# Summing the heads' logits on VectorE by way of DRAM instead of with selector matmuls, in a kernel bound by TensorE

## Chip, cores, metric

One core of one Trainium2 chip. The metric is device time in microseconds (us); lower is better. The engines are called PE (TensorE), DVE (VectorE), ACT (ScalarE), POOL (GpSimd) and SP (the engine whose queue starts the DMA transfers). "Starts" of matmuls below are start times in the trace. Full-width matmuls (128 rows, 128 columns, 512 moved columns, bf16) that nothing delays start 216 ns apart, and eight of them make a group of 1.73 us. A **PE wait** is what a gap between two starts has beyond 216 ns; gaps of 432 ns where the trace lacks the record of one matmul (about every fiftieth of `acc_wo` and `dacc` in some profiles) are not counted.

## The reference

Two rounds of the same two layers on x of 2048 tokens by 1024 features, all bf16: a dilated sliding-window attention (32 heads of 32, window 8, dilation 2) and a gated MLP with 3584 hidden features. Both have a layernorm ahead and a residual. (Shortened; `...` marks what is left out.)

```python
def _A_ref(x, wqkv, wo):                 # H = 32, Dh = 32, W, dil = 8, 2
    q, k, v = ...                        # x @ wqkv, split by heads
    idx = pos[:, None] - (jnp.arange(W) * dil)[None, :]
    kg, vg = ...                         # k and v gathered at idx
    logits = jnp.einsum("bhsd,bhswd->bhsw", q, kg) * scale   # masked where idx < 0
    attn = softmax(logits, axis=-1)
    o = jnp.einsum("bhsw,bhswd->bhsd", attn, vg)
    return o.transpose(0, 2, 1, 3).reshape(B, S, D) @ wo

def _B_ref(x, W_gate, W_up, W_down):
    gate, up = x @ W_gate, x @ W_up
    return (relu(gate) * up) @ W_down

for _ in range(2):
    x = x + _A_ref(layernorm(x), wqkv, wo)
    x = x + _B_ref(layernorm(x), W_gate, W_up, W_down)
```

## The kernel before

A block is 512 tokens in one of the two rounds, so there are eight, numbered n = 0 to 7. PE goes through the stages in a fixed order: in the first part v of blocks 0 to 3, q and k of blocks 0 and 1, and the output projection of block 0; then for each n the gate/up stage of block n (28 pairs of groups `acc_g`, `acc_u`), q and k of block n+2 (from block 4 on also v), the output projection `acc_wo` of block n+1, and the down projection `dacc` of block n. The attention of block n+1 runs on DVE while PE does gate/up of block n. q and k are laid out with four features of each head next to one another on the 128 partitions. DVE multiplies q with shifted k and sums over eight chunks; then the four partitions of one head have to be added. Before, this was a matmul with a 0/1 matrix `sel` of 32 columns, in tiles of 128 by 32 (all code below is shortened; `...` marks larger cuts):

```python
psum   = tc.tile_pool(name="psum", bufs=6, space=PSUM)      # six accumulators, tag "acc"
psum_l = tc.tile_pool(name="psum_l", bufs=1, space=PSUM)    # two banks, for the logits L

def dv(f, *args, **kwargs):          # fixes DVE's order: behind the last one issued so
    with tc.issue_after(tail_dve[0]):
        tail_dve[0] = f(*args, **kwargs).ins

def red_mm(n, prod, first, last):    # eight selector matmuls
    for wh in range(2):
        for tq in range(TPB):
            mm(st["L"][32 * tq:32 * tq + 32, WH * wh:WH * (wh + 1), :], lhsT=sel[:],
               rhs=prod[:, WH * wh:WH * (wh + 1), tq * P:(tq + 1) * P],
               start=first, stop=last, tile_position=(0, 32 * tq), ...)
# block 0: one red_mm per chunk, eight groups. Blocks 1 to 7: DVE sums the chunks into s, one red_mm.

def softmax(n):
    nc.vector.tensor_reduce(m[:], Lt..., op=ALU.max)
    nc.vector.tensor_tensor(d[:], Lt[:], m..., op=ALU.subtract)
    nc.scalar.activation(d[:], d[:], ACT.Exp, scale=scale)
    nc.vector.tensor_reduce(ssum[:], d..., op=ALU.add)
    nc.vector.reciprocal(rs[:], ssum[:])
    nc.vector.tensor_tensor(a[:], d[:], rs..., op=ALU.mult)

# pv_steps: eight units of four DVE operations each: tt = a * v, three halving adds into ohm

# gate/up, step j of 28
for nm in ("g", "u"):
    acc = psum.tile([P, BLK], F32, tag="acc", name=f"acc_{nm}")
    ...                                                   # eight matmuls
    if nm == "g":
        r = pool["hid"].tile([P, BLK], BF16, tag="r", name="r", bufs=3)
        tail_act[0] = nc.scalar.activation(r[:], acc[:], ACT.Relu).ins
nc.vector.tensor_tensor(hold["hT"][:, j, :], accs["u"][:], r[:], op=ALU.mult)   # frees acc_u

# down projection
if s8 == 0:
    accs[half] = [psum.tile([P, BLK], F32, tag="acc", name=f"dacc{t}") for t, _, _ in cols]

# the plan for gate/up of block n >= 1 ("at" is the stage's start in planned us)
ev.append((at + 0.1, reds_n[n + 1]))
ev.append((at + 0.2, lambda n=n: softmax(n + 1)))
spread(pv_steps(n + 1), at + 12.0, 6.5)
```

The product hT(j) on DVE is what gives an up group's accumulator back to PE, and the ReLU on ACT is what gives a gate group's back. DVE's operations without `dv` are ordered by the scheduler at build time, which interleaves two units where it can.

Of the kernel before, what the change touches and what calls it, by code (L numbers as in the profile page):

```python
# [17 lines left out]
W = 8  # L18
# [18 lines left out]
def kernel(  # L37
# [117 lines left out]
    v_d = dram.tile([H * DH, NTOK], BF16, name="v_d")  # L155
    o_d = dram.tile([NT, H, DH, P], BF16, name="o_d")
    zpad = const.tile([P, KC, HALO], BF16, name="zpad")
    nc.gpsimd.memset(zpad[:], 0.0)
# [145 lines left out]
    def ln_first():  # L304
# [55 lines left out]
        def turn(t):  # L360
            tps[t] = psum.tile([P, KC, P], BF16, tag="acc", name="tp")
            for c in range(KC):
                with pe_group():
                    tail_pe[0] = nc.tensor.transpose(tps[t][:, c, :], xna[:, t, c * P:(c + 1) * P], ident[:]).ins

        def copy(t, eng, c0=0, c1=KC):
            f = nc.vector.tensor_copy if eng == "v" else nc.scalar.copy
            on(eng, f, hold["xnT"][:, t, c0:c1, :], tps[t][:, c0:c1, :])

# [12 lines left out]
        apply(1)  # L382
        copy(0, "v", 0, KC // 2)
        copy(0, "a", KC // 2, KC)
        turn(1)
        act_vpe(2, st1)
        copy(1, "v", 0, KC // 2)
        copy(1, "a", KC // 2, KC)
        bn(3, 0)
# [3 lines left out]
        apply(3)  # L393
        hold["later"] = {2: (lambda: (turn(2), copy(2, "a"))),
                         4: (lambda: (turn(3), copy(3, "v", 0, KC // 2), copy(3, "a", KC // 2, KC)))}
        return hold
# [109 lines left out]
    def prod_direct_steps(n):  # L506
        prods = {}

        def mult(c):
            def f():  # L510
                prods[c] = work.tile([P, W, BLK], BF16, tag="t", name=f"prod_{c}")
                i0, i1 = qk_bcast(n, c, 0, W)
                dv(nc.vector.tensor_tensor, prods[c][:], i0, i1, op=ALU.mult)
            return f

        def red(c):
            def f():
                red_mm(n, prods.pop(c), c == 0, c == KC - 1)
            return f

        return [mult(c) for c in range(KC)], [red(c) for c in range(KC)]

    def prod_sum_steps(n):
        st = att[n]

        def mult(h, c):
            def f():
                if h == 0 and c == 0:
                    st["s"] = big_tile([P, W, BLK], f"s_{n}")
                i0, i1 = qk_bcast(n, c, WH * h, WH)  # L530
                if c == 0:
                    t = work.tile([P, WH, BLK], F32, tag="ac", name=f"ac_{n}_{h}", bufs=1)
                    st["ac"] = t
                else:
                    t = work.tile([P, WH, BLK], F32, tag="t", name=f"t_{n}_{h}_{c}")
                    st[("t", c)] = t
                behind = gate[0] if n == 1 else down_gate[0] if n == 2 else None
                if behind is not None:
                    with tc.issue_after(behind):
                        nc.vector.tensor_tensor(t[:], i0, i1, op=ALU.mult)  # L540
                else:
                    nc.vector.tensor_tensor(t[:], i0, i1, op=ALU.mult)  # L542
                if c > 1:
                    add(h, c - 1)
                if c == KC - 1:
                    add(h, c)
            return f

        def add(h, c):
            ac, t = st["ac"], st.pop(("t", c))  # L550
            o = st["s"][:, WH * h:WH * (h + 1), :] if c == KC - 1 else ac[:]
            nc.vector.tensor_tensor(o, ac[:], t[:], op=ALU.add)  # L552

        def red():
            red_mm(n, st["s"], True, True)

        return [mult(h, c) for h in range(2) for c in range(KC)], red

    def softmax(n):
        st = att[n]  # L560
        Lt = st["L"]
        if n % NB == 0:
            reg = Lt[0:32, :, 0:HALO]
            nc.vector.tensor_tensor(reg, reg, maskc[:], op=ALU.add)
        m = soft.tile([P, P], F32, tag="m", name="m")
        nc.vector.tensor_reduce(m[:], Lt[:].rearrange("p w t -> p t w"), axis=AX.X, op=ALU.max)
        d = soft.tile([P, W, P], F32, tag="d", name="d")
        nc.vector.tensor_tensor(d[:], Lt[:], _ap(m, 0, [[0, W], [1, P]]), op=ALU.subtract)
        nc.scalar.activation(d[:], d[:], ACT.Exp, scale=scale)
        ssum = soft.tile([P, P], F32, tag="ssum", name="ssum")  # L570
        nc.vector.tensor_reduce(ssum[:], d[:].rearrange("p w t -> p t w"), axis=AX.X, op=ALU.add)
        rs = soft.tile([P, P], F32, tag="rs", name="rs")
        nc.vector.reciprocal(rs[:], ssum[:])
        a = soft.tile([P, W, P], BF16, tag="a", name=f"a_{n}", bufs=2)
        nc.vector.tensor_tensor(a[:], d[:], _ap(rs, 0, [[0, W], [1, P]]), op=ALU.mult)
        st["a"] = a

# [14 lines left out]
    def pv_steps(n):  # L592
# [3 lines left out]
        def f_(g):  # L596
            def f():
# [5 lines left out]
                v_sh = _ap(st["v_hm"], HALO + g * DG * (HALO + P), [[-DIL, W], [HALO + P, DG], [1, P]])  # L603
                nc.vector.tensor_tensor(tt[:], a_bc, v_sh, op=ALU.mult)  # L604
                nc.vector.tensor_tensor(tt[:, 0:4], tt[:, 0:4], tt[:, 4:8], op=ALU.add)  # L605
                nc.vector.tensor_tensor(tt[:, 0:2], tt[:, 0:2], tt[:, 2:4], op=ALU.add)
                gate[0] = nc.vector.tensor_tensor(ohm[:, g * DG:(g + 1) * DG, :], tt[:, 0], tt[:, 1], op=ALU.add).ins
            return f
# [46 lines left out]
    def gu_steps(n, ln):  # L655
        hold = {}

        def f_(j):
            def f():
# [4 lines left out]
                for nm in ("g", "u"):  # L664
# [6 lines left out]
                    if nm == "g":  # L671
                        r = pool["hid"].tile([P, BLK], BF16, tag="r", name="r", bufs=3)
                        tail_act[0] = nc.scalar.activation(r[:], acc[:], ACT.Relu).ins  # L673
                nc.vector.tensor_tensor(hold["hT"][:, j, :], accs["u"][:], r[:], op=ALU.mult)  # L674
            return f

        return [f_(j) for j in range(FC)], hold

    down_gate = [None]

    def down_steps(n, hold):
        b = n % NB
        accs = {}

        def f_(half, s8):
            def f():
                hT = hold["hT"]
                cols = [(t, 0, SLAB) for t in range(TPB)]
                if n == NN - 1 and half == 1:
                    cols[-1:] = [(TPB - 1, 0, SLAB // 2), (TPB - 1, SLAB // 2, SLAB)]  # L690
                if s8 == 0:
                    accs[half] = [psum.tile([P, BLK], F32, tag="acc", name=f"dacc{t}") for t, _, _ in cols]
                ac = accs[half]
# [8 lines left out]
                if s8 == NSL - 1:  # L702
                    for a, (t, c0, c1) in zip(ac, cols):
                        xt = x_tiles[b * TPB + t]
                        xs = xt[:, half * SLAB + c0:half * SLAB + c1]
                        ins = nc.vector.tensor_tensor(xs, a[:, c0:c1], xs, op=ALU.add).ins  # L706
                        if n == 0 and half == 0:
                            down_gate[0] = ins
                        if n == NN - 1:
# [26 lines left out]
    ln_b = {}  # L736
    reds_n = {}
    ln_a[0] = ln_first()
# [22 lines left out]

    GAP0 = 2.05
    t_v0 = 9.5
# [25 lines left out]
    for c in range(KC):  # L789
        ev.append((t_qk0 + GAP0 * (2 * c + 2.0), mults[c]))  # L790
        if c < KC - 2:
            ev.append((t_qk0 + GAP0 * (2 * c + 4.5), reds[c]))
    spread(load_v_steps(0), t_qk0 + 19.0, 1.0)
    ev.append((t_qk1 + 0.5 * GRP, reds[KC - 2]))
    ev.append((t_qk1 + 2.5 * GRP, reds[KC - 1]))
    ev.append((t_qk1 + 2.6 * GRP, lambda: softmax(0)))
    ln1(2, t_qk0 + 10.0, t_qk1 + 5.0, True, 4.5)
    spread(qk_steps(1, ln_a[1], "qk01"), t_qk1, GRP)
# [8 lines left out]
    ev.append((t_wo0 + 3.0, store_v(2)))  # L807
    sums1, red1 = prod_sum_steps(1)
    spread(sums1[:4], t_qk1 + 50.0, 4.4)
# [6 lines left out]
    spread(load_v_steps(1), t_gu0 + 6.0, 7.0)  # L816
    ev.append((t_gu0 + 58.1, red1))
    ev.append((t_gu0 + 58.2, lambda: softmax(1)))
    ev.append((t_gu0 - 0.01, start_hidden))

    at = t_gu0
    for n in range(NN):
# [3 lines left out]
        if n == 0:  # L826
            spread(pv_steps(1), at + 66.0, 5.5)
            ev.append((at + 105.0, store_o(1)))
            ev.append((at + 105.1, load_o(1)))
        elif n + 1 < NN:  # L830
            ev.append((at + 0.1, reds_n[n + 1]))
            ev.append((at + 0.2, lambda n=n: softmax(n + 1)))
            spread(pv_steps(n + 1), at + 12.0, 6.5)
            ev.append((at + 72.0, store_o(n + 1)))
            ev.append((at + 72.1, load_o(n + 1)))
        if n + 2 < NN:
            ln1(n + 2, at + 30.0, at + 58.0)
        at += 2 * GRP * FC
        if n + 2 < NN:
            want_qk(("qk", n + 2), at + 2 * GRP * KC)  # L840
            spread(qk_steps(n + 2, ln_a[n + 2], ("qk", n + 2)), at, GRP)
            sums, reds_n[n + 2] = prod_sum_steps(n + 2)
            spread(sums, at + GRP * (K_STEP[0] + 1.0), 4.4)
            at += 2 * GRP * KC
# [51 lines left out]
```

## Time and profile before

1629.85 us, median of four runs beside the changed kernel (1629.76 to 1630.19); 1629.79 in the runs that were there first. The profiled execution spans 1628.1 us.

| profile before | |
|---|---|
| PE busy | 1617.5 us, 99% |
| DVE busy | 1062.6 us, 65% |
| DMA queue q1 | 63.4% of 16 engines, 295 MB |
| first `acc_v` of the real work | 9.99 us (it waits for a weight load) |
| last matmul to the end | about 3.6 us |
| selector matmuls | 120, in 15 groups of eight |

From the page of the kernel before, its head, the first lines of its parts 1 and 4, the clock and the DMA queue:

```profile
span 1628.1 us, 18770 instructions
PE 1617.5 (99%) x7617; PEld 784.6 (48%) x7666; DVE 1062.6 (65%) x927; ACT 506.0 (31%) x1050; POOL 255.9 (16%) x220
...
PEclk9999999999999999999999999999999999999999
...
q1 hardware_dynamic: 371808, 295.23, 63.4%
...
PE 95%; DVE 4%; issue 1%; DMA 0%; SPq 0%; DVEq 0%
```

PE is busy 99% at full clock, and the chain that ended last runs over PE for 95%. Time is to be had only from PE: fewer matmuls, or fewer waits. The Trainium skill, "Trainium Kernel Development and Optimization", Performance Expectations, calls matmul busy time a bad metric because matmuls are pipelined. This trace agrees: a matmul is shown as 379 ns long and starts 216 ns after the one before it. All PE waits below are therefore read from starts.

The timeline of PE before, around one group of selector matmuls (block 1; columns: start, length of the run, engine, line, operation, tiles, count):

```profile
198.78 1.03 PE L129 MATMUL acc_u<-xnT_b,w_u 128*128 128x512 bf16 x4
199.73 0.61 PE L129 MATMUL L<-s,sel 128*32 128x512 bf16 x8
200.28 1.90 PE L129 MATMUL acc_g<-xnT_b,w_g 128*128 128x512 bf16 x8
```

From the first L matmul to the next group is 0.55 us, and the first L matmul itself starts 0.31 us after the last `acc_u` one, 0.09 more than usual: the group costs 0.65 us (0.64 by the rounded lines).

The timeline of PE before, in the down projection of block 0 (in brackets the idle time and what ended it):

```profile
305.83 1.67 PE L129 MATMUL dacc<-w_d,hT 128*128 128x512 bf16 x7
308.28 2.96 PE L129 MATMUL dacc<-w_d,hT 128*128 128x512 bf16 x12 [0.77 <-DVE x L706]
```

Seven matmuls should take 1.51 us from start to start and took 2.45: a wait of 0.94 us for an accumulator that DVE has not yet read. It is the largest PE wait after the start.

The DVE and then the ACT timeline before, at the start of gate/up of block 1 (`m` is the maximum over L, `d` is L minus m, then the Exp of `d` on ACT, `ssum` is the sum after it):

```profile
333.33 1.22 DVE L566 TENSOR_REDUCE m<-L 128x128 f32<-128x1024 f32 x1
334.58 1.22 DVE L568 TENSOR_TENSOR d<-L,m 128x1024 f32<-128x1024 f32 x1
336.82 0.69 DVE L674 TENSOR_TENSOR hT<-acc_u,r 128x512 bf16<-128x512 f32 x1 [1.02 <-PE acc_u L129]
337.43 1.91 DVE L571 TENSOR_REDUCE ssum<-d 128x128 f32<-128x1024 f32 x1
```

```profile
335.03 0.60 ACT L673 ACTIVATE r<-acc_g 128x512 bf16<-128x512 f32 x1 [3.51 <-PE acc_g L129]
335.83 1.06 ACT L569 ACTIVATE d<-d 128x1024 f32<-128x1024 f32 x1 [0.21 <-DVE d L568]
```

`d` is ready at 335.80, and the Exp starts at 335.83, after only 0.21 us in which ACT was idle: it stands after two ReLUs in ACT's order, just where its data comes.

### The profile page before, as it was taken

How to read it: one execution, taken by the hardware profiler on the slowest of the kernel's cores; microseconds unless marked ns; L12 is line 12 of the kernel's file. 1: busy time of each engine (PE TensorE's matmuls, PEld its weight loads, DVE VectorE, ACT ScalarE, POOL GpSimd, SP SyncE). 2: the span in 40 equal slices, each digit the busy share in tenths (PEclk: the TensorE clock that was granted, in tenths of full speed). 3: DMA queues.
4: the chain of work that ended last, by engine and by line, in shares of the span. 5: the costliest groups of instructions: out<-in, count | busy, mean ns of one | idle time of the engine just before them, and what ended most of it. 6: DMA issues, size and time to landing. Idle time of an engine off the chain costs nothing.

```text
span 1628.1 us, 18770 instructions
## 1 busy us (share of the span) xinstructions
PE 1617.5 (99%) x7617; PEld 784.6 (48%) x7666; DVE 1062.6 (65%) x927; ACT 506.0 (31%) x1050; POOL 255.9 (16%) x220
## 2 busy tenths in 40 slices
PE   9999999999999999999999999999999999999999
PEld 5644445444544445444454444544445444444444
DVE  5699899985497927949279492894818958211211
ACT  4754323243241513405134051331513311131110
POOL 2421003310250102201052010520105100000000
PEclk9999999999999999999999999999999999999999
DMA  9579656747476485664857648577484764655452
GB/s 304 91 203 256 164 175 201 193 156 196 140 215 175 155 233 168 184 177 149 230 180 185 185 150 224 165 200 215 147 229 158 198 203 155 206 160 177 156 167 67
DMA packets 372183, 296.83 MB, mean 182 GB/s; under 512 B 142592, under 2 KB 352896, under 8 KB 371200
## 3 DMA queue, kind: packets, MB, share of 16 engines
q1 hardware_dynamic: 371808, 295.23, 63.4%
q8 instruction: 60, 0.98, 0.3%
q10 hardware_dynamic: 288, 0.39, 0.1%
q14 instruction: 27, 0.22, 0.0%
HBM read 256.77 MB, written 21.00 MB: 171 GB/s over the span
## 4 chain that ended last, share of the span: by engine, by line
PE 95%; DVE 4%; issue 1%; DMA 0%; SPq 0%; DVEq 0%
PE acc_g L129 24%; PE acc_u L129 24%; PE dacc L129 22%; PE acc_v L129 7%; PE acc_k L129 6%; PE acc_q L129 6%; PE acc_wo L129 6%; DVE t L542 1%; DVE ac L552 1%; PE L L129 1%; DMA w_v<-in_A_wqkv_dram 0%; DVE pv L604 0%; DVE x L649 0%; DVE pv L605 0%; DVE ac L542 0%
## 5 line engine op out<-in xcount | busy, mean ns | idle before, releaser
L129 PE MATMUL acc_g<-xnT_b,w_g 128*128 128x512 bf16 x1792 | 423.4, 379 | 0.0
L129 PE MATMUL acc_u<-xnT_b,w_u 128*128 128x512 bf16 x1792 | 423.3, 379 | 0.0
L129 PE MATMUL dacc<-w_d,hT 128*128 128x512 bf16 (+1 forms) x1787 | 386.6, 376 | 2.5 <-DVE x L706 0.8
L673 ACT ACTIVATE r<-acc_g 128x512 bf16<-128x512 f32 x224 | 133.4, 596 | 747.1 <-PE acc_g L129 747.1
L674 DVE TENSOR_TENSOR hT<-acc_u,r 128x512 bf16<-128x512 f32 x224 | 153.7, 687 | 315.0 <-PE acc_u L129 313.5
L129 PEld LDWEIGHTS <-hT 128*128 128x128 bf16 x1820 | 178.0, 98 | 209.9 <-issue 1.1
L129 PEld LDWEIGHTS <-w_g 128*128 128x128 bf16 x1792 | 174.8, 98 | 212.8 <-issue 3.0
L129 PEld LDWEIGHTS <-w_u 128*128 128x128 bf16 x1792 | 175.3, 98 | 211.4
L552 DVE TENSOR_TENSOR ac<-ac,t 128x2048 f32<-128x2048 f32 x84 | 191.7, 2282 | 0.4
L542 DVE TENSOR_TENSOR t<-q,k 128x2048 f32<-128x2048 bf16 x81 | 184.8, 2290 | 8.5 <-ACT k L480 5.8
L485 POOL COPY kh<-k 128x14 bf16<-128x14 bf16 x64 | 81.4, 1276 | 472.0 <-ACT k L480 471.8
L706 DVE TENSOR_TENSOR x<-dacc,x 128x512 bf16<-128x512 f32 (+1 forms) x65 | 42.5, 679 | 164.0 <-PE dacc L129 164.0
L604 DVE TENSOR_TENSOR pv<-a,vhm 128x4096 bf16<-128x4096 bf16 x64 | 145.2, 2282 | 0.0
L129 PE MATMUL acc_wo<-w_o,oT 128*128 128x512 bf16 x496 | 111.0, 379 | 0.8
L245 POOL TENSOR_TENSOR st_b<-st_b,neg_half 128x1 f32<-128x1 f32 x29 | 56.5, 1956 | 288.7 <-ACT st_b L244 288.6
L245 POOL TENSOR_TENSOR st_a<-st_a,neg_half 128x1 f32<-128x1 f32 x32 | 41.9, 1316 | 319.2 <-ACT st_a L244 319.1
L484 POOL COPY k<-kh 128x14 bf16<-128x14 bf16 x48 | 70.5, 1469 | 65.9 <-DVE t L542 43.8
L129 PEld LDWEIGHTS <-oT 128*128 128x128 bf16 x512 | 50.1, 98 | 60.3
L605 DVE TENSOR_TENSOR pv<-pv 128x2048 bf16<-128x2048 bf16 x64 | 77.4, 1215 | 0.2
L476 ACT CAST q<-acc_q 128x512 bf16<-128x512 f32 x64 | 37.3, 583 | 73.3 <-PE acc_q L129 73.2
L240 ACT ACTIVATE xn_b<-x 128x1024 bf16<-128x1024 bf16 x29 | 30.3, 1045 | 89.3 <-DVE x L649 89.3
L480 ACT CAST k<-acc_k 128x512 bf16<-128x512 f32 x64 | 37.3, 583 | 63.0 <-PE acc_k L129 62.8
(131 smaller groups left out, 1214.1 us busy)
## 6 DMA issues: line engine op xcount, KB each, us to landing
w_g<-in_B_W_gate_dram SPq DMA_DIRECT2D x56, 1024.0 KB, 6.7
w_u<-in_B_W_up_dram SPq DMA_DIRECT2D x56, 1024.0 KB, 5.4
w_d<-in_B_W_down_dram SPq DMA_DIRECT2D x48, 1024.0 KB, 5.8
w_o<-in_A_wo_dram SPq DMA_DIRECT2D x16, 1024.0 KB, 7.2
vhm<-v_d SPq DMA_DIRECT2D x32, 284.0 KB, 6.9
v_d<-vT SPq DMA_DIRECT2D x8, 1024.0 KB, 10.1
oT<-o_d SPq DMA_DIRECT2D x32, 256.0 KB, 4.5
w_d<-in_B_W_down_dram SPq DMA_DIRECT2D x16, 512.0 KB, 4.0
```

Source lines behind the costliest of these rows:

```text
L129: tail_pe[0] = nc.tensor.matmul(*args, **kwargs).ins
L245: nc.gpsimd.tensor_tensor(rstd, vpe, neg_half[:, 0:1], op=ALU.pow)
L476: tail_act[0] = nc.scalar.copy(q[:], acc[:]).ins
L484: nc.gpsimd.tensor_copy(k[:, 0:HALO], khalo[n - 1][:, c, :])
L485: nc.gpsimd.tensor_copy(khalo[n][:, c, :], k[:, BLK:BLK + HALO])
L542: nc.vector.tensor_tensor(t[:], i0, i1, op=ALU.mult)
L552: nc.vector.tensor_tensor(o, ac[:], t[:], op=ALU.add)
L604: nc.vector.tensor_tensor(tt[:], a_bc, v_sh, op=ALU.mult)
L605: nc.vector.tensor_tensor(tt[:, 0:4], tt[:, 0:4], tt[:, 4:8], op=ALU.add)
L673: tail_act[0] = nc.scalar.activation(r[:], acc[:], ACT.Relu).ins
L674: nc.vector.tensor_tensor(hold["hT"][:, j, :], accs["u"][:], r[:], op=ALU.mult)
L706: ins = nc.vector.tensor_tensor(xs, a[:, c0:c1], xs, op=ALU.add).ins
```

## The change

The intent: take selector matmuls off PE, and fix DVE's order so that its new work falls where it was planned.

1. Blocks 2 to 7: `s` goes to DRAM and comes back with the heads on the partitions; DVE adds the four features (the "head sum", two operations), and no selector matmul is left there.
2. DVE's products hT, softmax and PV are put in a fixed order (`dv`), in units of four PV operations.
3. Block 0: two groups of 32 selector matmuls instead of eight of eight.
4. Two of the four accumulators of a down projection's second half come from the L banks.
5. The transposes at the start go to two half-size tiles, with other engines for some copies.

Three small things go with it: an order rule for block 2's sums (`down_gate`) is dropped, most products of block 0 come from another buffer pool, and the store and load of the attention's output move 8 us later in the plan.

The core of the diff (`GRP` is the planned time of a group, `GAP0` that of a q/k step of block 0, `at` and `t_...` are planned times in us):

```diff
+    s_d = [dram.tile([P, W * BLK], BF16, name=f"s_d{i}") for i in range(2)]
... (first transposes: two half tiles, copies by halves)
-        return [mult(c) for c in range(KC)], [red(c) for c in range(KC)]
+        return [mult(c) for c in range(KC)], [red(0, KC // 2), red(KC // 2, KC)]
...
+    def store_s(n):
+        def f():
+            sp_dma(s_d[n % 2][:], att[n]["s"][:].rearrange("p w t -> p (w t)"))
+    def load_s(n):                      # four loads, runs of P = 128 bf16
+            ...
+                src = bass.AP(tensor=sd.tensor, offset=sd.offset + tq * P,
+                              ap=[[DG * W * BLK, H], [BLK, DG * W], [1, P]])
+                sp_dma(s4[32 * tq:32 * tq + 32, :, :, :].rearrange("p d w t -> p (d w) t"), src)
+    def head_sum(n):
+        dv(nc.vector.tensor_tensor, u[:], s4[:, 0:2], s4[:, 2:4], op=ALU.add)
+        dv(nc.vector.tensor_tensor, u[:, 0], u[:, 0], u[:, 1], op=ALU.add)
+        return u[:, 0]
-    def softmax(n):
+    def softmax_steps(n):               # three steps: shift, exps, norm
+            Lt = st["L"][:] if n < 2 else head_sum(n)
...  (nc.vector.X(...) becomes dv(nc.vector.X, ...) in softmax, PV and hT; the Exp is not ordered)
-                nc.vector.tensor_tensor(hold["hT"][:, j, :], accs["u"][:], r[:], op=ALU.mult)
+                dv(nc.vector.tensor_tensor, hold["hT"][:, j, :], accs["u"][:], r[:], op=ALU.mult)
...
+                    if half == 1:
+                        pair = psum_l.tile([P, TPB // 2, BLK], F32, tag="L", name="dacc_pair")
+                        own = {2: pair[:, 0, :], 3: pair[:, 1, :]} if len(cols) == TPB else {2: pair[:, 0, :]}
...
-            ev.append((at + 0.1, reds_n[n + 1]))
-            ev.append((at + 0.2, lambda n=n: softmax(n + 1)))
-            spread(pv_steps(n + 1), at + 12.0, 6.5)
+            ev.append((at - 3.1, store_s(n + 1)))
+            ev.append((at + 0.4, load_s(n + 1)))
+            spread(softmax_steps(n + 1), at + 14.0, 3.6)
+            spread(pv_steps(n + 1), at + 25.0, 6.5)
... (the plan of blocks 0 and 1 moved by a few us)
```

## The prediction

> **What bounds it now.** TensorE. The page has PE busy 1617.5 of 1628.1 us, PEclk full in every slice; the chain of waits gives PE 95%. In the PE timeline full-width matmuls start every 216 ns; the 7424 useful ones make about 1602 us (estimate). The rest of the span: 10.0 us before the first acc_v (it waits for the w_v load), about 3.5 us of tail, and about 12 us of other PE work. DVE (65%) and DMA (63%) hide. Only PE time counts.
>
> **What the change takes from PE.**
> - Selector matmuls (L) of blocks 2 to 7. By start-to-start times, a group of eight costs 0.65 us beyond the neighbours' cadence: 2 x 0.216 streaming (four 32-column matmuls start 3 ns apart, then four more) plus about 0.22 for entering and leaving. The Trainium skill, "TensorEngine Tiling (Array Packing)", Key Properties, says that changing the tiling mode drains TensorE; the trace agrees: 309 ns between starts going in, 312 coming out, instead of 216. 6 x 0.65 = 3.9 us.
> - Block 0: eight L groups (0.70 us each there) become two of 32 matmuls; streaming stays, six changes go: 8 x 0.70 - 2 x (0.70 + 3 x 0.43) = 1.6 us.
> - One stall: at 308 us block 0's second half of the down projection waits for DVE (starts 1151 ns apart). Two accumulators in the free L banks remove it: 0.9 us.
> - Transposes: 0. The first acc_v starts when w_v lands, and PE has no gap after it.
>
> **What it adds, off the path (estimates from like shapes in the trace).** DVE: head sum 2.3 + 1.2 us in six blocks, 21 us. DMA: 1 MB out and back per block, 12 MB on 297, the way back in 256-byte runs like oT's. DVE order fixed in units: one PV unit is 2.28 + 1.21 + 0.68 + 0.41 = 4.6 us, and an hT product may wait that long; with six accumulators of 1.73 us each, PE tolerates about 8. DVE in a gate/up stage: 28 x 0.69 + 36.6 + 12 = 68 of 97 us: fits.
>
> **Latency checks.** s is ready before the gate/up stage starts (block 2: 323 against 329 us). Store (about 10 us, like ohm's) and load (5 to 7) end about 14 us into it; the head sum follows the fifth hT at about 18. Tightest is block 7: PV ends about 78 us into the stage, store 4 to 10, oT 5 to 7: 87 to 95; the output projection starts at 97. In block 0 prod 3 ends at about 43.2 us; its selector matmuls are due at about 43.6. I expect no stall over 0.5 us from either.
>
> **Prediction.** 1629.8 - 3.9 - 1.6 - 0.9 = 1623.4 us; 8 in 10: 1621.8 to 1626.4. Faster by over 2%: 0.003; within 2%: 0.987; slower: 0.01.
>
> **What would show it.** 72 L matmuls instead of 120, in three groups; no dacc wait of PE; start and tail unchanged; DVE about 20 us busier; DMA about 2 points higher; block 1's q/k about 2 us earlier, its gate/up stage 2.5.
>
> **What would make it wrong.** The store and load of s holding the DMA queue so that a weight slab comes late; the head sum holding hT past 8 us; block 7's oT late, stalling the last output projection; the 32-matmul groups waiting for products, or streaming slower. Each costs 1 to 5 us, none 2%.

## The result, and the profile after

The changed kernel took 1625.89 us, median of four runs (1625.71 to 1626.60), against 1629.85 of the kernel before. The ratio is 0.9976, 95% interval 0.9959 to 0.9993. A ratio here is the mean time of one kernel's fast runs over that of the other's of the same rounds, so it is not quite the ratio of the medians. All runs were at full clock, and every kernel but one was correct.

So 4.0 us came, where 6.4 were predicted. The time lies inside the predicted range, and in the class predicted, but 2.5 us of the expected gain are missing. It stayed inside because the range reached 3 us above the middle, not because the mechanism was right; the slowest of the four runs, 1626.60, is just outside (1626.4).

The same lines of the page after (the clock line is unchanged and left out):

```profile
span 1624.3 us, 18771 instructions
PE 1615.9 (99%) x7618; PEld 785.2 (48%) x7618; DVE 1100.5 (68%) x939; ACT 502.2 (31%) x1051; POOL 250.2 (15%) x220
...
q1 hardware_dynamic: 397632, 307.81, 67.1%
...
PE 88%; DVE 10%; issue 1%; DMA 1%; ACT 0%; POOL 0%; DVEq 0%; SPq 0%
```

PE is still busy 99%, but the chain that ended last now runs over DVE for 10% instead of 4%. That is the first sign: PE has begun to wait for DVE now and then.

The groups of selector matmuls by shape (columns: line, engine, operation, tiles, form, count, busy us, mean ns, idle before), before and then after:

```profile
L129 PE MATMUL L<-prod,sel 128*32 128x512 bf16 x64 | 4.9, 384 | 0.0
L129 PE MATMUL L<-s,sel 128*32 128x512 bf16 x56 | 4.3, 384 | 0.0
```

```profile
L129 PE MATMUL L<-prod,sel 128*32 128x512 bf16 x64 | 4.0, 381 | 0.1
L129 PE MATMUL L<-s,sel 128*32 128x512 bf16 x8 | 0.6, 384 | 0.0
```

The removal came as planned: 120 selector matmuls became 72, in three groups. The wait at 308 us is gone as well. What came new is in the waits. From the view of waits, before (us in all, times, longest), and then after:

```profile
DVE ssum L571 <- ACT d L569: 1.1, 1, 1.1
PE dacc L129 <- DVE x L706: 0.8, 1, 0.8
```

```profile
DVE ssum L103 <- ACT d L600: 31.8, 7, 5.2
ACT r L711 <- DVE hT L103: 27.4, 9, 4.6
PE acc_g L129 <- DVE hT L103: 1.2, 4, 0.3
PE acc_wo L129 <- DMA oT<-o_d: 0.3, 1, 0.3
```

DVE stands 5.2 us in front of `ssum` in each of six blocks, waiting for the Exp; ACT waits for hT; and PE's gate groups wait for hT. The timeline of PE after, in gate/up of block 1:

```profile
376.91 1.89 PE L129 MATMUL acc_u<-xnT_b,w_u 128*128 128x512 bf16 x8
379.11 1.89 PE L129 MATMUL acc_g<-xnT_b,w_g 128*128 128x512 bf16 x8 [0.31 <-DVE hT L103]
```

The starts are 2.20 us apart instead of 1.73, a wait of 0.47 us; the idle time in brackets shows only 0.31 of it. The same wait stands in gate/up of blocks 2, 3 and 4, always in front of the 16th gate group; in block 5 it is 0.41 in front of the 14th up group and 0.07 in front of the 16th gate group. Together they cost 2.4 us. In gate/up of block 6 there is none.

And its cause, upstream. The ACT timeline after, and then the DVE timeline after, in the same stage:

```profile
352.94 0.60 ACT L711 ACTIVATE r<-acc_g 128x512 bf16<-128x512 f32 x1 [2.86 <-PE acc_g L129]
356.39 0.60 ACT L711 ACTIVATE r<-acc_g 128x512 bf16<-128x512 f32 x1 [2.86 <-PE acc_g L129]
356.88 1.05 ACT L600 ACTIVATE d<-d 128x1024 f32<-128x1024 f32 x1
```

```profile
350.99 1.22 DVE L103 TENSOR_TENSOR d<-u,m 128x1024 f32<-128x1024 f32 x1
352.13 0.68 DVE L103 TENSOR_TENSOR hT<-acc_u,r 128x512 bf16<-128x512 f32 x1
357.96 1.91 DVE L103 TENSOR_REDUCE ssum<-d 128x128 f32<-128x1024 f32 x1 [5.15 <-ACT d L600]
359.91 0.95 DVE L103 RECIPROCAL rs<-ssum 128x128 f32<-128x128 f32 x1
360.90 1.23 DVE L103 TENSOR_TENSOR a<-d,rs 128x1024 bf16<-128x1024 f32 x1
362.04 0.69 DVE L103 TENSOR_TENSOR hT<-acc_u,r 128x512 bf16<-128x512 f32 x1
```

`d` is ready at 352.2, but the Exp starts at 356.88. It stands in ACT's order behind two more ReLUs, and those wait for gate groups that PE has not computed yet. The Exp could have run in ACT's idle 2.86 us. The Trainium skill, "PSUM — Partial Sum Buffer", Engine vs sequencer instructions, says that ScalarE's and VectorE's queues are strict FIFO. The trace agrees: 4.7 us between data and start, with ACT idle for most of it. On DVE, whose order the change fixes, the same holds for hT: from 352.13 to 362.04 no hT runs, though PE finishes an up group every 3.46 us; the up group of the next one was done at 354.63, while DVE stood idle until 357.96. From there on DVE has to catch up between PV units.

I call the **lateness** of a product hT(j) its start minus the end of the last matmul of its up group. In gate/up of blocks 1 to 6 the largest lateness was at most 3.3 us before, and is 9.9 us after, at j = 11.

The account, from the starts of the two profiles: 6.4 us predicted, and the first `acc_v` came 0.46 us earlier (9.53 for 9.99; other profiles of these kernels have 9.4 to 10.4); against these, new PE waits of 3.2 us: 2.4 in the gate/up stages, 0.47 at 112 us (`acc_wo` of block 0 waits for `oT`), 0.31 in the first selector group of block 0 (at 42.8 us, for the fourth product), 0.04 elsewhere. 6.4 + 0.46 - 3.2 is 3.7; the spans differ by 3.8.

### The profile page after: what moved, and what is told of

Same layout as the page of the kernel before. It is cut to its first block, busy times and chain, and to the rows that moved or that the text cites. A ratio compares the mean times of both kernels' runs of the same rounds, so it can differ in the third digit from the quotient of the medians.

```text
span 1624.3 us, 18771 instructions
## 1 busy us (share of the span) xinstructions
PE 1615.9 (99%) x7618; PEld 785.2 (48%) x7618; DVE 1100.5 (68%) x939; ACT 502.2 (31%) x1051; POOL 250.2 (15%) x220
## 4 chain that ended last, share of the span: by engine, by line
PE 88%; DVE 10%; issue 1%; DMA 1%; ACT 0%; POOL 0%; DVEq 0%; SPq 0%
PE acc_g L129 21%; PE acc_u L129 20%; PE dacc L129 18%; PE acc_wo L129 7%; PE acc_q L129 6%; DVE pv L103 6%; PE dacc_pair L129 6%; PE acc_k L129 5%; PE acc_v L129 5%; DVE hT L103 1%; DVE ssum L103 1%; DMA x<-in_A_x_dram 1%; DVE prod L103 1%; DVE bst L103 0%; ACT d L600 0%
## 5 line engine op out<-in xcount | busy, mean ns | idle before, releaser
L103 DVE TENSOR_TENSOR hT<-acc_u,r 128x512 bf16<-128x512 f32 x224 | 150.0, 687 | 237.7 <-PE acc_u L129 235.5
L129 PE MATMUL dacc<-w_d,hT 128*128 128x512 bf16 (+1 forms) x1400 | 301.6, 375 | 0.0
L547 DVE TENSOR_TENSOR t<-q,k 128x2048 f32<-128x2048 bf16 x84 | 191.8, 2292 | 8.7 <-ACT k L482 5.8
L748 DVE TENSOR_TENSOR x<-dacc,x 128x512 bf16<-128x512 f32 (+1 forms) x50 | 32.1, 676 | 158.1 <-PE dacc L129 158.1
L103 DVE TENSOR_TENSOR pv<-pv 128x2048 bf16<-128x2048 bf16 (+1 forms) x128 | 122.7, 959 | 4.4
L246 POOL TENSOR_TENSOR st_a<-st_a,neg_half 128x1 f32<-128x1 f32 x32 | 49.4, 1551 | 390.7 <-ACT st_a L245 390.7
L129 PE MATMUL dacc_pair<-w_d,hT 128*128 128x512 bf16 x420 | 95.9, 379 | 0.0
L246 POOL TENSOR_TENSOR st_b<-st_b,neg_half 128x1 f32<-128x1 f32 x29 | 47.6, 1650 | 289.9 <-ACT st_b L245 289.9
L478 ACT CAST q<-acc_q 128x512 bf16<-128x512 f32 x64 | 37.3, 583 | 75.3 <-PE acc_q L129 75.3
```

Source lines behind the costliest of these rows:

```text
L129: tail_pe[0] = nc.tensor.matmul(*args, **kwargs).ins
L246: nc.gpsimd.tensor_tensor(rstd, vpe, neg_half[:, 0:1], op=ALU.pow)
L478: tail_act[0] = nc.scalar.copy(q[:], acc[:]).ins
L547: nc.vector.tensor_tensor(t[:], i0, i1, op=ALU.mult)
L748: nc.vector.tensor_tensor(xs, a[:, c0:c1], xs, op=ALU.add)
```

## The experiments

Theories for the missing 2.5 us:

- **A**: the Exp stands too late in ACT's order; with DVE's order fixed, its wait makes hT late, and PE waits for the accumulator that the late hT holds.
- **B**: the head sum (3.5 us more DVE work in front of the Exp) makes hT late.
- **C**: the next block's layernorm on ACT (from 363.8 us, just after the lines of ACT shown above) makes the ReLUs late, and through them hT.
- **D**: the waits in block 0 (selector group, `oT`) are what costs.

Twelve kernels ran, each timed in five rounds beside the kernel before, whose median was 1629.74 to 1629.91 in all of them. "After" below is the changed kernel.

### Theory A, the Exp: run e1

After, with the Exp of blocks 2 to 7 issued ahead of the eighth ReLU. Only ACT's order changes.

```diff
-            nc.scalar.activation(d[:], d[:], ACT.Exp, scale=scale)
+            exp_ins[n] = nc.scalar.activation(d[:], d[:], ACT.Exp, scale=scale).ins
...
-                        tail_act[0] = nc.scalar.activation(r[:], acc[:], ACT.Relu).ins
+                        late = tc.issue_after(exp_ins[n + 1]) if j == 7 and 1 <= n < NN - 1 else nullcontext()
+                        with late:
+                            tail_act[0] = nc.scalar.activation(r[:], acc[:], ACT.Relu).ins
```

> Only the ScalarE order changes: the Exp of the softmax of blocks 2 to 7 stands after 7 ReLUs of its gate/up stage instead of after 9. Theory A (the Exp stood behind ReLUs that had to wait for their gate matmuls, VectorE sat idle 5.15 us before the softmax sum, its fixed order kept the hT products behind it, and TensorE ran out of accumulators): the wait before the sum falls from 5.15 to about 1.1 us, the largest lateness of an hT product from 9.9 to about 6 us, the five TensorE waits of about 0.47 us in the gate/up stages of blocks 1 to 5 vanish; about 2.4 us less than the changed kernel, so about 1623.5 us. Theory B (the VectorE work itself, that is the head sum and the PV units of 4.6 us placed ahead of hT products, makes hT late) and theory C (the layernorm statistics on ScalarE delay the ReLUs): the waits stay, 1625.9 us.

Measured: 1623.52 us (1623.31 to 1624.96), ratio 0.9964, 95% interval 0.9951 to 0.9976; that is 2.4 below after, and its span is 2.7 below after's. Lines of its waits, then of its ACT timeline and of its PE timeline:

```profile
DVE ssum L103 <- ACT d L602: 4.3, 7, 1.1
```

```profile
351.91 1.06 ACT L602 ACTIVATE d<-d 128x1024 f32<-128x1024 f32 x1 [2.17 <-DVE d L103]
352.87 0.58 ACT L715 ACTIVATE r<-acc_g 128x512 bf16<-128x512 f32 x1
```

```profile
376.57 1.89 PE L131 MATMUL acc_u<-xnT_b,w_u 128*128 128x512 bf16 x8
378.30 1.89 PE L131 MATMUL acc_g<-xnT_b,w_g 128*128 128x512 bf16 x8
```

The Exp now starts as soon as its data is there, DVE's wait in front of `ssum` fell from 31.8 us in all to 4.3, the lateness from 9.9 to 5.3 us (5.6 in one stage), and the starts on PE are 1.73 us apart again. All waits of PE for hT are gone. (One of 0.23 us is new in this profile, in front of the first gate group of block 0 at 139 us; e2 and e12 have it too.) The ReLU of the 13th gate group, behind the layernorm, is 4.5 us late in e1 as in after, so a late ReLU alone does not make these waits. Theory A holds.

Run e3 below will show that an edit can also change which accumulator a group gets, so the built programs were checked for this too: in that of e1, the accumulator of the 12th up group is used again after seven groups in blocks 1 to 5, as in after. What removed the wait in e1 is the lateness.

### Theory B, the head sum: run e2

After, without the second of the two additions. The result is wrong (relative error 0.67); the DVE work in front of the Exp is 1.2 us less.

```diff
-        dv(nc.vector.tensor_tensor, u[:, 0], u[:, 0], u[:, 1], op=ALU.add)
```

> Wrong on purpose: the second add of the head sum (1.22 us of VectorE, six times) is left out, so the logits miss half of the sum; orders of all engines otherwise as in the changed kernel, the Exp still after 9 ReLUs. Theory A: the Exp waits for the ninth ReLU anyway, so the sum starts as before, the wait before it grows by 1.2 to about 6.4 us, the TensorE waits stay near 0.47 us per stage, time within 0.3 us of 1625.9. Theory B: hT comes 1.2 us earlier, more than the 0.47 us that TensorE waits, so the waits vanish and the time falls to about 1623.5 us.

Measured: 1626.75 us (1626.12 to 1627.75), ratio 0.9983 (0.9969 to 0.9996). The wait in front of `ssum` grew to 35.7 us in all (5.8 at the longest, where I had expected 6.4): of the 1.2 us that DVE saves in a block, 0.6 are spent waiting there and 0.6 in front of an hT ahead of it, as the Exp stands where it stood. The lateness stays 9.9 us. The time is 0.9 above after, where I had expected it within 0.3: there is one PE wait more, 0.47 us in gate/up of block 6. As a sufficient cause B falls. The extra wait puzzled me until run e3.

### Theory C, the layernorm: run e3

After, with the next block's layernorm planned 20 us later; in the trace of block 1 it starts after 15 ReLUs, at 379.2 us, where it started after 11, at 363.8. (The expectation says after the fourteenth.)

```diff
-            ln1(n + 2, at + 30.0, at + 58.0)
+            ln1(n + 2, at + 50.0, at + 78.0)
...
-                with (tc.issue_after(tail_act[0]) if early else nullcontext()):
+                with (tc.issue_after(tail_act[0]) if early or which == "a" else nullcontext()):
```

> The layernorm of the next attention block on ScalarE starts after the fourteenth ReLU of the gate/up stage instead of after the eleventh, and is emitted 20 us later, with its transposes. Theory A: the idle time before the softmax sum stays 5.15 us, the lateness of hT stays 9.9 us; the TensorE waits stay near 0.47 us per stage, 1625.9 us. Theory C: the ReLUs are on time, the waits vanish, about 1623.5 us. If the waits shrink but hT stays 9.9 us late, both are needed.

Measured: 1624.62 us (1623.45 to 1625.09), ratio 0.9967 (0.9955 to 0.9980). That is 1.3 below after by the medians and 2.6 by the spans of the profiles (1621.7 for 1624.3; the profiled run was the fastest of five), so the size is not settled. A miss for me: I had expected the waits to stay, and they went, although the lateness is 9.9 us still, DVE's wait in front of `ssum` is 32.0 us in all, and ACT waits for hT 75.2 us instead of 27.4. So the layernorm isn't what makes hT late, and lateness alone doesn't make PE wait.

What had changed is which accumulator each group gets. That is decided when the kernel is built, and it is not a plain rotation. In the built program of after, in blocks 1 to 5, the 16th gate group gets the accumulator of the 12th up group, **seven** groups after it; in block 6, where there is no wait at the same lateness, that accumulator goes to the 16th up group, **eight** groups later. In e3 it is eight in blocks 1 to 5 too. In e2, block 6 has seven, and has the wait. Block 5 of after shows a third case: there the 14th up group uses the accumulator of the 11th again, six groups later; that hT is 8.1 us late, and PE waits 0.41 us. (In these the accumulators are read from the built programs, not from a trace.) So theory A got a second half: how late hT may be depends on when its accumulator is used again. Runs e9, e10 and e12 test that.

### Theory D, block 0: run e4

After, with the first selector group of block 0 one step later, and PV of block 0 in interleaved pairs as the scheduler had it before.

```diff
-    ev.append((t_qk0 + GAP0 * 9.5, reds[0]))
+    ev.append((t_qk0 + GAP0 * 10.5, reds[0]))
...
-    spread(pv_steps(0), t_qk1 + 12.0, 4.2)
+    spread(pv_steps(0), t_qk1 + 12.0, 8.4)    # block 0: pairs of units, operations taking turns
```

> Two edits in block 0. The first selector group of 32 matmuls stands one q/k step later, so that product 3 is ready; and PV of block 0 runs two units side by side, as the kernel before did, so that VectorE does not wait for its own last result between dependent operations. Expected: the 0.31 us gap inside the first selector group is gone, PV of block 0 ends about 2 to 3 us earlier (37.3 us from first to last operation become about 34.5), and the 0.47 us wait for oT before the first output projection is gone: 0.8 us less than the changed kernel, about 1625.1 us, with the five waits in the gate/up stages unchanged. Rival: TensorE only runs on to the next late product or load, and the waits reappear there; 1625.9 us.

Measured: 1625.73 us (1625.07 to 1626.96), ratio 0.9976 (0.9964 to 0.9989). In its profile both waits of block 0 are gone and the span is 0.9 us below after's (1623.3); the gate/up waits are as in after. The timed median is only 0.2 us lower, which is inside the spread. So these waits exist in the profile of after and are absent with the edit, but that the edit saves time is not shown. They also come and go without it: with block 0 as in after, the selector wait is in the profile of after alone, and the `oT` wait in those of after, e3 and e9, but not of e1, e2 and e12.

### Both repairs together, and the three savings one by one: runs e5 to e8

Run e5 is after with the edits of e1 and e4.

> The changed kernel with the early Exp of the first experiment and the two block 0 edits of the fourth. If the waits are separate causes, their savings add: no TensorE wait on hT in the gate/up stages, no gap in the first selector group, no wait for oT in block 0; 1629.8 - 3.9 - 1.6 - 0.9, and nothing given back, so 1623.4 less the 0.4 us by which the first acc_v has started earlier in most profiles: about 1622.8 us. If block 0's edits only move a wait, it equals the early-Exp kernel, 1623.5 us.

Measured: 1623.53 us (1623.36 to 1623.65), ratio 0.9962 (0.9949 to 0.9974). The PE waits after the first `acc_v` sum up to 0.1 us. This version beats both kernels: 6.2 us below before and 2.4 below after. It is equal to e1 by timing, so the 1622.8 that I had expected did not come: e4's edits added nothing that the timing shows, though from the first `acc_v` to the end of the span e5 is 0.4 shorter than e1. With the waits gone, each predicted saving can be undone alone.

Run e6 is e5 with the selector matmuls back in blocks 2 to 7.

```diff
-            ev.append((at - 3.1, store_s(n + 1)))
-            ev.append((at + 0.4, load_s(n + 1)))
+            ev.append((at + 12.0, lambda n=n: red_mm(n + 1, att[n + 1]["s"], True, True)))
...
-            Lt = st["L"][:] if n < 2 else head_sum(n)
+            Lt = st["L"][:]
```

> The combined kernel with one part undone: the logits of blocks 2 to 7 come again from eight selector matmuls per block, placed 12 us into the gate/up stage, without DRAM and without the head sum. By the forecast's term of 0.65 us per group on TensorE: 6 x 0.65 = 3.9 us more than the combined kernel, 1626.6 us, with 309 and 312 ns between starts going in and out of each group. If the way through DRAM costs time elsewhere (DMA contention, late weights), the difference is smaller than 3.9.

Measured: 1627.16 us (1626.69 to 1628.07), ratio 0.9985 (0.9972 to 0.9997): 3.6 more than e5, and 4.0 more by the spans (1625.7 for 1621.65). Predicted 3.9. So the way through DRAM costs nothing that shows on PE.

Run e7 is e5 with all accumulators of the down projection from the common six (`if half == 1:` made `if False:`).

> The combined kernel with one part undone: the second half of the down projection takes its four accumulators from the six common ones again. By the forecast: the one TensorE wait of about 0.9 us on VectorE at the second half of block 0's down projection (near 303 us) comes back, and nothing in the other blocks; 0.9 us more than the combined kernel, 1623.7 us. If VectorE's new order has its adds done in time there, no difference.

Measured: 1624.42 us (1623.96 to 1625.00), ratio 0.9968 (0.9955 to 0.9982): 0.9 more than e5 by timing, predicted 0.9. Its profile has one PE wait, 1.21 us, at the place of the old one, and is 1.2 longer from the first `acc_v` to the end.

Run e8 is e5 with eight selector groups in block 0 again, at the places of the kernel before but for the last, which is one q/k step earlier.

```diff
-    ev.append((t_qk0 + GAP0 * 10.5, reds[0]))
+    for c in range(KC - 2):
+        ev.append((t_qk0 + GAP0 * (2 * c + 4.5), reds[c]))
...
-    ev.append((t_qk1 + 1.5 * GRP, reds[1]))
+    ev.append((t_qk1 + 0.5 * GRP, reds[KC - 2]))
+    ev.append((t_qk1 + 1.5 * GRP, reds[KC - 1]))
```

> The combined kernel with one part undone: the selector matmuls of block 0 in eight groups again, at the places of the kernel before. By the forecast 1.6 us more than the combined kernel, 1624.4 us: eight groups of 0.70 us instead of two of 2.0. If streaming inside the groups of 32 is slower than 216 ns per four matmuls, the difference is smaller.

Measured: 1624.54 us (1624.44 to 1625.93), ratio 0.9970 (0.9957 to 0.9982): 1.0 more than e5 by timing; from first `acc_v` to the end of the span it is 1.6 more. Predicted 1.6. The profile agrees with the prediction, and the timed medians leave the size between 1.0 and 1.6.

### The size of the wait: runs e9 and e10

If A is right, a later Exp must cost in proportion. Run e9 is after with one more ACT operation in front of the Exp, which changes nothing in the result:

```diff
+            if n > 1:
+                nc.scalar.activation(d[:], d[:], ACT.Identity)
             nc.scalar.activation(d[:], d[:], ACT.Exp, scale=scale)
```

> The changed kernel with one more ScalarE operation (the identity on d, in place, about 1.05 us) in front of the Exp of blocks 2 to 7; the result doesn't change, nor do the orders on TensorE and VectorE, nor the accumulators that the build gives in stages 1 to 5. Theory A (the Exp's late place in ScalarE's order makes the hT products late, and TensorE waits where they are later than the accumulator's reuse allows): the largest lateness of hT grows from 9.9 to about 10.9 us, the wait of acc_g in the gate/up stages of blocks 1 to 4 from 0.47 to 1.3 to 1.6 us each, the last stage has none: about +4 to +5 us, 1630 to 1631 us. Rival (the waits are something else that ends at the same place, such as the layernorm or the DMA): waits and time as before, 1626.

Measured: 1631.69 us (1631.27 to 1631.93), ratio 1.0012 (0.9998 to 1.0025), 5.8 above after and a little above the expected 1630 to 1631 (the gate/up waits of the profile account for 5.4). One ScalarE operation of 1.05 us in six blocks takes the whole gain of the change away. Its DVE and its PE timelines:

```profile
359.31 1.92 DVE L103 TENSOR_REDUCE ssum<-d 128x128 f32<-128x1024 f32 x1 [6.25 <-ACT d L602]
```

```profile
377.17 1.89 PE L129 MATMUL acc_u<-xnT_b,w_u 128*128 128x512 bf16 x8
380.47 1.89 PE L129 MATMUL acc_g<-xnT_b,w_g 128*128 128x512 bf16 x8 [1.41 <-DVE hT L103]
```

DVE waits 6.25 us instead of 5.15. The largest lateness is 11.0 us instead of 9.9, and the PE wait 1.56 us in each of five stages (3.30 between the starts, less 1.73), where it was 0.47 in four of them. (In block 5 the edit changed the accumulators too, against my expectation: the 11th up group's is used again after seven groups instead of six, so all five waits of e9 are at the 16th gate group.) Both cases give the same tolerance: 9.93 - 0.47 and 11.02 - 1.56 are both 9.46 us (the expectations have it as 9.4). With block 5 of after (8.14 - 0.41, six groups) that makes 7.73 us for six groups and 9.46 for seven, one group of 1.73 us apart. In gate/up of block 6, where the accumulator is used again eight groups later, there is no wait even at 11.0.

Run e10 has the same operation, but in e5, where there is room.

> The same extra operation of about 1.05 us in front of the Exp, but in the combined version, where the Exp stands after seven ReLUs. Theory A with a tolerance of about 9.4 us of lateness: hT's lateness grows from 5.3 to about 6.4 us, stays under the tolerance, no wait on TensorE, 1623.5 us within 0.5. If the operation cost time by itself (ScalarE near its limit), it would be 1625 or more.

Measured: 1623.87 us (1623.07 to 1624.36), ratio 0.9963 (0.9951 to 0.9976). The lateness rose from 5.3 to 6.4 us (6.7 in one stage, from 5.6), under the tolerance (the accumulator of the 12th up group is again used after seven groups in blocks 1 to 5), and no gate/up stage waits for hT. One wait of 0.54 us in its profile is for a load of `w_o`. So the operation costs nothing by itself; what it costs in e9 is the wait.

### The transposes: run e11

Run e11 is e5 with the first transposes and copies as they were before the change.

> The combined version with the first transposes and their copies as they were before the change. The prediction gave this part of the change 0 us: 1623.5 us within 0.3, and the first acc_v starts within the spread of the other profiles (9.5 to 10.2 us). If the paired tiles gain something, this is slower by up to 0.5 us.

Measured: 1623.52 us (1623.26 to 1624.27), ratio 0.9962 (0.9949 to 0.9976), the same as e5. The first `acc_v` starts at 10.4 us in its profile, a little outside the spread that I had named. By timing, this part of the change gives nothing, as predicted.

### The accumulators alone: run e12

After, with DVE, PE and DMA in the same order (on ACT one normalisation moves by one ReLU), and the accumulators assigned by hand. In the gate/up stages the gate groups take turns on two, the up groups on four; all other groups take them in rotation.

```diff
+    def acc_tile(shape, dtype, name):
+        turn_of[0] += 1
+        two = turn_of[0] % 3 == 0
+        return psum.tile(shape, dtype, tag="two" if two else "acc", name=name, bufs=2 if two else 4)
... (everywhere but in gate/up: psum.tile(..., tag="acc", ...) becomes acc_tile(...))
-                    acc = psum.tile([P, BLK], F32, tag="acc", name=f"acc_{nm}")
+                    acc = psum.tile([P, BLK], F32, tag="two" if nm == "g" else "acc", name=f"acc_{nm}",
+                                    bufs=2 if nm == "g" else 4)
```

> The changed kernel with its instruction orders kept (TensorE, VectorE and DMA the same; on ScalarE one normalisation moves by one ReLU), and only the accumulators assigned by hand: in the gate/up stages the gate groups take turns on two, the up groups on four, so that an up group's accumulator is used again eight groups later, never seven. Theory A in its refined form (what TensorE can bear is set by when the accumulator of a late product is used again): hT is still 9.9 us late at the 12th product, but the tolerance for up groups rises from 9.4 to about 11.1 us, so the waits of 0.47 us in five gate/up stages go: about 1623.5 us, 2.4 below the changed kernel. A gate group now comes back four groups later, and a ReLU 4.5 us late just fits: if it doesn't, small waits of up to 0.1 us remain. Rival (lateness of hT over about 9.4 us stops TensorE whatever accumulator is used, or the waits have another source): the waits stay, 1626.

Measured: 1624.62 us (1623.27 to 1624.94), ratio 0.9964 (0.9951 to 0.9978); 1.3 below after by median, with a span 1.4 below. Its DVE and its PE timelines:

```profile
358.01 1.91 DVE L110 TENSOR_REDUCE ssum<-d 128x128 f32<-128x1024 f32 x1 [5.15 <-ACT d L607]
```

```profile
373.50 1.89 PE L136 MATMUL acc_u<-xnT_b,w_u 128*128 128x512 bf16 x8
375.35 1.89 PE L136 MATMUL acc_g<-xnT_b,w_g 128*128 128x512 bf16 x8
377.07 1.89 PE L136 MATMUL acc_u<-xnT_b,w_u 128*128 128x512 bf16 x8
378.80 1.89 PE L136 MATMUL acc_g<-xnT_b,w_g 128*128 128x512 bf16 x8
```

DVE waits 5.15 us as before the edit, and hT is 9.9 us late in all six stages. Yet the wait of 0.47 us in front of the 16th gate group (at 378.80) is gone. In its place stands the small one that I had feared: 0.12 us in front of the 15th (375.35 is 1.85 after 373.50), in five stages, where a gate group now has to wait for a late ReLU (that of the 13th gate group ends at 375.30). The profile has 0.5 us of other single waits, one of them in front of the first gate group at 139 us; with the five small ones that is most of the 1.2 us by which its span is above e5's. The expected 1623.5 was not reached. So the same lateness costs 0.47 us or nothing, depending only on when the accumulator comes round.

### All runs

| run | what | median us | against before | largest lateness of hT, us | gate/up waits of blocks 1 to 6, us |
|---|---|---|---|---|---|
| after | the change | 1625.89 | 0.9976 | 9.9 | 2.4 |
| e1 | Exp earlier | 1623.52 | 0.9964 | 5.6 | 0 |
| e2 | shorter head sum (wrong result) | 1626.75 | 0.9983 | 9.9 | 2.8 |
| e3 | layernorm later | 1624.62 | 0.9967 | 9.9 | 0 |
| e4 | block 0 repaired | 1625.73 | 0.9976 | 9.9 | 2.4 |
| e5 | e1 and e4 | 1623.53 | 0.9962 | 5.6 | 0 |
| e6 | e5, selector matmuls in 2 to 7 | 1627.16 | 0.9985 | 4.0 | 0 |
| e7 | e5, no accumulators from L | 1624.42 | 0.9968 | 5.6 | 0 |
| e8 | e5, eight groups in block 0 | 1624.54 | 0.9970 | 5.6 | 0 |
| e9 | after, Exp 1.05 us later | 1631.69 | 1.0012 | 11.0 | 7.8 |
| e10 | e5, Exp 1.05 us later | 1623.87 | 0.9963 | 6.7 | 0 |
| e11 | e5, old transposes | 1623.52 | 0.9962 | 5.6 | 0 |
| e12 | after, accumulators by hand | 1624.62 | 0.9964 | 9.9 | 0.6 |

## Why the prediction was right or wrong

**The removed PE work: right.** 3.9 us for the selector matmuls of blocks 2 to 7 (undone alone: 3.6 timed, 4.0 by spans), 0.9 for the accumulator wait (0.9 timed, 1.2 by the profile), 1.6 for block 0 (1.0 timed, 1.6 by the profile), 0 for the transposes (0). Their basis was one cost per group, 0.65 to 0.70 us, of which 0.43 is matmul streaming and the rest, about 0.22 to 0.27, the changing of tile shape. The Trainium skill, "TensorEngine Tiling (Array Packing)", Key Properties, says that changing the mode drains TensorE; the trace agrees with 309 ns between starts on the way in and 312 on the way out, instead of 216. With all waits mended, e5 takes 1623.53 us: the forecast of 1623.4 was the time of the change without its defect.

**"an hT product may wait that long" (4.6 us, one PV unit): wrong, and this is the step that failed.** The term was zero in the sum and is 2.4 us. hT does wait about 4.7 us behind a PV unit, but it waits 9.9 in the worst place, because I sized DVE's fixed order by DVE's own work. The softmax has a step on ACT in its middle. I did not ask where that step stands in ACT's order, and it stands behind two ReLUs that wait for PE: 5.15 us of idle DVE in front of `ssum`, with hT shut out by the fixed order. (That a free order of DVE would have let hT through is not tested; the runs move the Exp and the accumulators.) Before the change the scheduler had ordered DVE freely and the Exp came after two ReLUs.

**"PE tolerates about 8": about right for what it assumed, wrong in kind.** I took six accumulators in rotation, and 7.7 us is what the trace gives where an accumulator is used six groups later. But the build doesn't rotate plainly: it is 9.5 us where it is seven groups, and over 11.0 where it is eight. The lateness of 9.9 fell between the last two, so five of six stages wait and one doesn't.

**"The head sum holding hT past 8 us": the right result, named among the risks, for the wrong reason.** With a head sum 1.2 us shorter the lateness was unchanged (e2).

**"I expect no stall over 0.5 us from either" (block 7's oT, block 0's selector group): held.** Block 7's projection didn't wait. Block 0's first group waited 0.31 us in the profile of after, and in none of the others. A wait of 0.47 us for block 0's `oT` was not foreseen: its PV in dependent order took 37.3 us instead of 34.3, as one unit takes 4.67 us alone. e4 removes both; that they matter to the timed runs is not shown.

**Transfers: right.** The store of s took 8.4 us at the median (estimate: about 10), a load 6.7 (estimate: 5 to 7), and PE never waited for them. DMA rose by 3.7 points, not 2. DVE became 38 us busier, not 20: 21.0 are the head sum as costed, about 4 are the maximum, 1.91 us each over the head sum for 1.22 over L. The operations' own times add up to only 28 us more; the other 10 are overlap that was lost: the page counts it once where two operations overlap, and 614 of 927 operations started before the one ahead had ended, 474 of 939 after.

**The landmarks**: gate/up of block 1 began 2.2 us earlier (329.00 to 326.84), where 2.5 were predicted, and its q/k 2.4 earlier (56.65 to 54.30), where 2 were predicted. Both contain the 0.46 us of the earlier start.

## What to carry to other kernels

When you fix the order of one engine, also follow every step of the chain that runs on another engine, and look at what stands in front of it in that engine's queue. Here one Exp behind two ReLUs too many cost 2.4 us, and one queue edit on ACT gave it back. On a bound engine, cost a delay as lateness against tolerance: below the tolerance a microsecond of delay costs nothing (e10), above it the full microsecond in every stage (e9), and the tolerance is set by how many groups later the build uses the same accumulator again. Assignments that the build makes can change with an unrelated edit (e2, e3, e9), so check them before you credit an edit with an effect.

## What the Trainium skill lacked or had wrong

- "TensorEngine Tiling (Array Packing)", Key Properties: states the drain at a mode change but no cost. Here it is about 0.09 us each way, 309 and 312 ns between starts instead of 216, and a group of eight 128 by 32 matmuls costs 0.65 us in all.
- "PSUM — Partial Sum Buffer", Engine vs sequencer instructions: the FIFO is stated and holds, but not what it means across engines. An Exp whose data was ready at 352.2 us started at 356.9, behind two ReLUs, and held DVE for 5.15 us.
- "Perfetto Trace Analysis", Matmuls: says that matmul groups should rotate through the banks. Which rotation matters: used again after six groups, a late reader was tolerated for 7.7 us; after seven, for 9.5; after eight, for at least 11.0.
- "Trainium Kernel Development and Optimization", Performance Expectations: the warning about matmul busy time is right, but gives no size. Here PE showed 99% busy before and after, with 3.2 us of new waits; a gap of 0.47 us in the starts showed as 0.31 us idle.
